# Fronts beside four plain MLP groups, then eight groups with both MLP layers as Strassen's seven products: one change to a lightning-attention and Fourier-mix kernel

## The chip, the cores and the metric

The kernel runs on one core of a Trainium2 chip. The metric is the device time of one execution in microseconds (us), lower is better. Three runs before the change took 942.44, 943.5 and 944.67 us; the median is 943.5 us.

## The reference, cut to what matters

B is 4 sequences of S = 768 rows, H = 8 heads of D = 64, so that the bridge gives x of 4 x 768 x 512. All is float32.

```
# attention, in blocks of 64 rows, a state per head carried along
intra = (q_b k_b^T * Dmask) v_b ;  inter = (q_b * lam^(i+1)) state
state = lam^64 * state + (k_b * rev_pow)^T v_b
x     = heads side by side                      # 4 x 768 x 512
# Fourier mix and MLP
u  = x + real(fft2(x))                          # over the 768 rows and 512 columns
un = (u - mean(u)) / sqrt(var(u) + 1e-6)
out = u + max(un @ w1, 0) @ w2                  # w1: 512 x 2048, w2: 2048 x 512
```

## The kernel before, in words

**Fronts.** For each sequence b a front makes the input of the MLP. `attn_chunk` works on 128 rows at a time (NC = 6 chunks): three loads, transposes of k and q (L259, L264), scores (L277), the state (L292 to L297), the output (L305, L309) and its transposes (L316). PSUM tiles of the fronts come from the pool `pa` with 5 buffers. `fft_ln` then writes and gathers mirrored rows through DRAM (`mirror_a`, `mirror_b`, L364 to L372), folds them on VectorE (`fold_a`, `fold_b`, L352 to L403), does the transform over rows (L427) and over columns (`width`, L440 to L445), adds it to x (L490, L491) and, for each of the three groups of a sequence, normalizes (`norm`: L457 to L469), transposes (L473) and copies the result to `ut` (L474). `ut` has 2 buffers, the row tiles `x` have 10. A group g is the pair of 128-row tiles (g, 3 + g); the groups come in the order 1, 2, 0.

**MLP.** `mlp(b)` goes over the three groups of a sequence. Layer 1 (L513): 16 chunks of 128 hidden units, each the sum of 4 products of 128x128 weights with 128x256 of `ut`; ReLU alternates between ScalarE (L521) and VectorE (L519) and fills the tiles `hr`. Layer 2 (L527): for both row tiles 16 products of a 128x128 of `hr` with 128x512 of w2. Two additions (L533, L534) make `y`, which is stored plainly or, for the upper row tile, scattered (L538). PSUM of the MLP comes from the pool `pm` with 3 buffers. Every matmul of the program stands as two instructions in the trace, since it is float32.

**Order.** Front and MLP are generators that yield a guessed cost after each step. `weave(lead, other, ratio)` writes the program: after each step of `lead` it takes steps of `other` until their cost is `ratio` times that of the lead. The Tile framework then plans the order on each engine ahead of time: among the instructions whose inputs and buffers its own model has ready, it takes the one that was written first, and each engine runs its queue in that order. Front 0 is woven with the conversion of the weights, its transform with front 1, the rest of front 1 with the MLP of sequence 0 (ratio 1.5). Fronts 2 and 3 are each woven with the MLP of the sequence ahead (`0.9 * t_mlp / t_front`, about 2.0); the MLP of sequence 3 stands alone.

Of the kernel before, what the change touches and what calls it, by code (L numbers as in the profile page):

```python
# [75 lines left out]
def kernel(  # L76
# [25 lines left out]
    G = 2  # L102
    NG = NC // G
    TT = [(t, HC + t) for t in range(HC)]
# [5 lines left out]
    ld = ctx.enter_context(tc.tile_pool(name="ld", bufs=2))  # L110
    at = ctx.enter_context(tc.tile_pool(name="at", bufs=1))
    xp = ctx.enter_context(tc.tile_pool(name="xp", bufs=2 * NC - 2))
    xn = ctx.enter_context(tc.tile_pool(name="xn", bufs=HC))
    fp = ctx.enter_context(tc.tile_pool(name="fp", bufs=1))
    np_ = ctx.enter_context(tc.tile_pool(name="np", bufs=2))
    ep = ctx.enter_context(tc.tile_pool(name="ep", bufs=2))
    hp_ = ctx.enter_context(tc.tile_pool(name="hp", bufs=FO // 4 + 1))
    dram = ctx.enter_context(tc.tile_pool(name="dram", bufs=1, space=bass.MemoryType.DRAM))
    PS = bass.MemoryType.PSUM
    pa = ctx.enter_context(tc.tile_pool(name="pa", bufs=5, space=PS))  # L120
    pm = ctx.enter_context(tc.tile_pool(name="pm", bufs=3, space=PS))
# [21 lines left out]
    n, b2 = 1, 0  # L143
    while n < C:
# [3 lines left out]
        n, b2 = 2 * n, b2 + 1  # L148
# [21 lines left out]
    for g in range(0, H, 4):  # L170
        ps = psum_m([C, 4, C])
# [12 lines left out]

    cs = const.tile([128, 2, 2, 2, NK], F32, name="cs")
    dt = const.tile([128, 5, QM + 1], F32, name="dt")
    ix = const.tile([128, 2 + HC * (B + 1)], U32, name="ix")

    def row_of(j, n=128):
        return bass.IndirectOffsetOnAxis(ap=ix[0:n, j:j + 1], axis=0)  # L190

    w1 = const.tile([128, KO, DFF], F32, name="w1")
    w2 = const.tile([128, FO, DM], F32, name="w2")

    w1v = moe_w_ch1.rearrange("(c p) f -> p c f", p=128)
    w2v = moe_w_ch2.rearrange("(c p) m -> p c m", p=128)
# [42 lines left out]
    xs, xn_, xd = {}, {}, {}  # L239
# [95 lines left out]

    uts = {}
# [75 lines left out]
    def fft_ln(b):  # L414
# [7 lines left out]
        for i in range(5):  # L422
            ps = psum_a([128, 2, NK])
            m = 128 if i < 4 else 1
            for n in range(2):
                for a, rows in enumerate(BLK):
                    mm = nc.tensor.matmul(ps[0:m, n, :], lhsT=piece(a, i, n), rhs=cs[0:rows, a, i in (2, 3), n, :],  # L427
                                          start=(a == 0), stop=(a == 1))
# [24 lines left out]
        def norm(g):  # L453
            mv = new(np_, [128, G, 2], "mv")
            for i in range(G):
                stt = new(np_, [128, 6], "stt")
                nc.vector.bn_stats(stt, xs[b, TT[g][i]])  # L457
                nc.vector.bn_aggr(mv[:, i, :], stt)
            ve = new(np_, [128, G], "ve")
            rs = new(np_, [128, G], "rs")  # L460
            nc.gpsimd.tensor_scalar(ve, mv[:, :, 1], EPS, None, op0=ALU.add)
            nc.gpsimd.tensor_tensor(rs, ve, mhalf, op=ALU.pow)
            yield 1.0
            ut = uts[b, g] = new(np_, [128, KO, G * 128], "ut")
            for i in range(G):
                un = new(np_, [128, DM], "un", bufs=1)
                u = xs[b, TT[g][i]]
                for o, x in ((un[:, 0:HM], u[:, 0:HM]), (un[:, HM:DM], u[:, DM - 1:HM - 1:-1])):
                    nc.vector.tensor_scalar(o, x, mv[:, i, 0:1], rs[:, i:i + 1],  # L469
                                            op0=ALU.subtract, op1=ALU.mult)  # L470
                pt = psum_a([128, KO, 128])
                for c in range(KO):
                    nc.tensor.transpose(pt[:, c, :], un[:, 128 * c:128 * c + 128], ident)  # L473
                nc.scalar.copy(ut[:, :, 128 * i:128 * i + 128], pt)  # L474
                yield 0.7

        for t in (1, 2, 0):
            ps = psum_a([128, DM])
# [3 lines left out]
            B = bs[t % 2]  # L482
# [6 lines left out]
            u, v_ = xs[b, t], xs[b, HC + t]  # L489
# [3 lines left out]
            if t == 0:  # L493
                ps = psum_a([128, DM])
# [8 lines left out]
            yield from norm(t)  # L503


    def mlp(b):
        for g in (1, 2, 0):
            ut = uts.pop((b, g))
            hr = []
            for fc in range(FO):  # L510
                ps = psum_m([128, G * 128])
                for c in range(KO):
                    nc.tensor.matmul(ps, lhsT=w1[:, c, 128 * fc:128 * fc + 128], rhs=ut[:, c, :],  # L513
                                     start=(c == 0), stop=(c == KO - 1))
                if fc % 4 == 0:
                    hr.append(new(hp_, [128, 4, G * 128], "hr"))
                t = hr[-1][:, fc % 4, :]
                if fc % 2:
                    nc.vector.tensor_scalar(t, ps, 0.0, None, op0=ALU.max)  # L519
                else:  # L520
                    nc.scalar.activation(t, ps, AF.Relu)  # L521
                yield 1.7
            for i in range(G):
                T = TT[g][i]
                ps = psum_m([128, DM])
                for fc in range(FO):
                    nc.tensor.matmul(ps, lhsT=hr[fc // 4][:, fc % 4, 128 * i:128 * i + 128], rhs=w2[:, fc, :],  # L527
                                     start=(fc == 0), stop=(fc == FO - 1))
                    if fc % 4 == 3 and fc < FO - 1:
                        yield 3.4  # L530
                u = xs.pop((b, T))
                y = new(np_, [128, DM], "y", bufs=1)
                nc.vector.tensor_tensor(y[:, 0:HM], ps[:, 0:HM], u[:, 0:HM], op=ALU.add)  # L533
                nc.vector.tensor_tensor(y[:, HM:DM], ps[:, HM:DM], u[:, DM - 1:HM - 1:-1], op=ALU.add)  # L534
                if T < HC:
                    nc.sync.dma_start(out[b, 128 * T:128 * T + 128, :], y)
                else:
                    nc.gpsimd.indirect_dma_start(out=out.rearrange("b s d -> (b s) d"),  # L538
                                                 out_offset=row_of(2 + HC * (b + 1) + T - HC),
                                                 in_=y[:, :], in_offset=None)  # L540
                yield 3.4
# [24 lines left out]
    def run(gen):  # L566
        return sum(gen)

    def part(gen, n):
        for d in gen:  # L570
            yield d
            n -= d
            if n <= 0:
                return

    NW = KO * DFF // WP
    w = weights()
    t_mlp = NG * (FO * 1.7 + G * 4 * 3.4)
    t_chunk = 7.3
    t_att, t_front = NC * t_chunk, NC * t_chunk + 10.0 + 7.0 + 5.7 + 3 * 2.4  # L580
    run(weave(attn(0), part(w, 0.5 * NW), 0.5 * NW / t_att))
# [9 lines left out]
    for b in range(B):  # L591
        back = mlp(b)
        if b == 0:

            run(weave(part(fr, 2 * t_chunk), weave(part(back, FO * 1.7 - 1.0), w, 0.9), 1.5))
            run(w)
# [34 lines left out]
```

## Time and profile before

| what | value |
|---|---|
| median of 3 runs | 943.5 us |
| the profiled execution, its own time | 942.13 us |
| its span, first to last instruction | 940.4 us |
| granted TensorE clock, mean of the span | 0.983 |
| matmul busy (PE) | 868.4 us |
| VectorE, ScalarE, GpSimd busy | 314.9, 184.7, 95.7 us |
| layer 1 matmuls (L513), layer 2 matmuls (L527) busy | 350.3, 336.8 us |
| DMA moved | 55.59 MB |

A group line of the page reads: line, engine, operation, output tile <- input tiles, shapes, count | busy time and mean of one | idle time of the engine ahead of them and what ended most of it. In a timeline a row is start, duration, engine, line, operation, count of merged instructions, and in brackets the idle time ahead of it with what ended it. The duration of merged matmuls reaches to the modelled end of the last, which overlaps the next row; distances between starts are used for rates. In the chain of waits a row is start, length, engine and line.

### The profile page before, as it was taken

The page shows a single profiled execution, that of the slowest core. Times are in us where ns is not written, and L with a number is a line of the kernel's source. Part 1 is how long each engine was busy: PE and PEld are TensorE (multiplying, and loading weights), DVE is VectorE, ACT ScalarE, POOL GpSimd, SP SyncE. Part 2 cuts the span into 40 slices and gives each one's busy share as a digit, 9 for nine tenths or more (in the row PEclk, how much of TensorE's full clock was granted, in tenths as well). Part 3 has the DMA queues.
Part 4 walks back from the last instruction along what each step waited for, and adds up shares of the span by engine and source line. Part 5 has one row for each costly group of instructions (what it writes and reads, how often), then busy time and mean ns, then how long its engine had stood idle before and what let it go on. Part 6 is the DMA issues. An engine that isn't in the chain of part 4 may idle for free.

```text
span 940.4 us, 10700 instructions
## 1 busy us (share of the span) xinstructions
PE 868.4 (92%) x4404; PEld 597.6 (64%) x4404; DVE 314.9 (33%) x694; ACT 184.7 (20%) x403; POOL 95.7 (10%) x108
## 2 busy tenths in 40 slices
PE   4766687699999999999999999999999999999997
PEld 2655576547747668668668558658668658485763
DVE  4779879843601011112243412111242401010100
ACT  3665346701100002112012001112002001000000
POOL 2225412000100001011100001010200000000000
PEclk9998889899999999999999999999999999999999
DMA  9798417500000011222200011221200000000000
GB/s 223 213 240 252 134 46 219 157 22 23 1 12 12 1 45 37 55 79 73 79 23 0 1 45 34 57 65 38 62 23 1 1 23 0 12 12 11 12 0 23
DMA packets 89272, 55.59 MB, mean 59 GB/s; under 512 B 76768, under 2 KB 78312, under 8 KB 89224
## 3 DMA queue, kind: packets, MB, share of 16 engines
q1 hardware_dynamic: 83264, 40.73, 16.5%
q0 software_dynamic: 2496, 7.87, 2.5%
q10 hardware_dynamic: 3464, 6.30, 1.8%
q8 instruction: 35, 0.57, 0.3%
q14 instruction: 13, 0.11, 0.0%
HBM read 42.29 MB, written 12.60 MB: 58 GB/s over the span
## 4 chain that ended last, share of the span: by engine, by line
PE 76%; DVE 10%; issue 4%; DMA 4%; ACT 2%; POOL 1%; POOLq 0%; SPq 0%; DVEq 0%; ACTq 0%
PE pm L527 32%; PE pm L513 29%; PE pa L427 3%; DMA raw<-in_moe_w_ch_dram 3%; PE pa L309 2%; PE pa L277 2%; PE pa L473 1%; PE pa L305 1%; PE pa L316 1%; DVE pw L222 1%; DVE stt L457 1%; DMA r<-xa,ix 1%; PE pa L292 1%; PE pa L264 1%; PE pa L259 1%
## 5 line engine op out<-in xcount | busy, mean ns | idle before, releaser
L513 PE MATMUL pm<-ut,w 128*128 128x256 f32 x1536 | 350.3, 383 | 9.8 <-ACT hr L521 8.0
L527 PE MATMUL pm<-w,hr 128*128 128x512 f32 x768 | 336.8, 594 | 0.0
L513 PEld LDWEIGHTS pm<-ut,w 128*128 128x128 f32 x1536 | 287.5, 191 | 54.9 <-ACT hr L521 8.7
L527 PEld LDWEIGHTS pm<-w,hr 128*128 128x128 f32 x768 | 143.7, 190 | 168.3 <-issue 167.4
L519 DVE TENSOR_SCALAR hr<-pm 128x256 f32<-128x256 f32 x96 | 40.7, 423 | 234.6 <-PE pm L513 234.3
L521 ACT ACTIVATE hr<-pm 128x256 f32<-128x256 f32 x96 | 36.7, 384 | 385.6 <-PE pm L513 354.1
L533 DVE TENSOR_TENSOR y<-pm,x 128x256 f32<-128x256 f32 x24 | 10.2, 425 | 234.9 <-PE pm L527 234.9
L538 POOL DMA_INDIRECT out_dram<-y,ix x12 | 12.1, 1009 | 344.0 <-DVE y L534 343.7
L255 POOL TENSOR_TENSOR kd<-k,decay 128x512 f32<-128x512 f32 x20 | 25.8, 1290 | 190.6 <-issue 110.7
L309 PE MATMUL pa<-sc,v 128*64 128x128 f32 x384 | 31.6, 292 | 10.5 <-DVE sc L281 10.5
L281 DVE TENSOR_TENSOR sc<-pa,decay 128x512 f32<-128x512 f32 x48 | 31.3, 685 | 24.8 <-PE pa L277 21.3
L277 PE MATMUL pa<-qT,kT 64*128 64x128 f32 x384 | 30.2, 298 | 8.9 <-ACT qT L266 8.9
L277 PEld LDWEIGHTS pa<-qT,kT 64*128 64x128 f32 x384 | 25.2, 199 | 18.1 <-ACT qT L266 11.9
L309 PEld LDWEIGHTS pa<-sc,v 128*64 128x64 f32 x384 | 23.5, 144 | 17.5 <-DVE sc L281 13.6
L269 DVE TENSOR_TENSOR qs<-pa,qpow 128x512 f32<-128x512 f32 x20 | 13.8, 691 | 48.4 <-ACT qT L266 48.4
L312 ACT COPY oT<-pa 128x512 f32<-128x512 f32 x24 | 14.1, 585 | 78.9 <-PE pa L309 78.9
L473 PE MATMUL pa<-ident,un 128*128 128x128 f32 x96 | 16.6, 294 | 13.6 <-DVE un L469 13.6
L261 ACT COPY kT<-pa 128x512 f32<-128x512 f32 x24 | 14.1, 588 | 72.5 <-PE pa L259 72.1
L220 ACT ACTIVATE pw<-pw,cvt 128x512 uint16<-128x512 uint16 x32 | 22.8, 719 | 17.1 <-DVE pw L219 17.1
L305 PE MATMUL pa<-qs,st 64*64 64x128 f32 x320 | 22.7, 283 | 3.2 <-DVE qs L269 3.1
L473 PEld LDWEIGHTS pa<-ident,un 128*128 128x128 f32 x96 | 11.3, 146 | 22.0 <-issue 12.4
L296 POOL TENSOR_TENSOR st<-st,qpow 128x256 f32<-128x256 f32 x16 | 22.5, 1406 | 19.0 <-DVE st L297 10.2
(94 smaller groups left out, 641.5 us busy)
## 6 DMA issues: line engine op xcount, KB each, us to landing
raw<-in_moe_w_ch_dram SPq DMA_DIRECT2D x32, 512.0 KB, 4.8
k<-in_k_dram SPq DMA_DIRECT2D x24, 256.0 KB, 3.4
q<-in_q_dram SPq DMA_DIRECT2D x24, 256.0 KB, 3.8
v<-in_v_dram SPq DMA_DIRECT2D x24, 256.0 KB, 3.1
out_dram<-y SPq DMA_DIRECT2D x12, 256.0 KB, 2.0
xa<-x ACTq DMA_DIRECT2D x8, 256.0 KB, 3.0
xa<-xn ACTq DMA_DIRECT2D x8, 256.0 KB, 4.4
xb<-xn ACTq DMA_DIRECT2D x8, 256.0 KB, 6.1
```

What stands on the lines that cost most here:

```text
L220: nc.scalar.activation(pw, pw, AF.Relu, bias=cvt[:, 0:1], scale=-1.0)
L255: nc.gpsimd.tensor_tensor(kd, kt, kpow, op=ALU.mult)
L277: mm(pss[hi][:, hp, :], lhsT=kT[HD[hi], hp, :], rhs=qT[HD[hi], hp, :], start=True, stop=True)
L281: nc.vector.tensor_tensor(t, pss[hi], decay[:, hi::2, :], op=ALU.mult)
L305: mm(po[HD[hi], hp, :], lhsT=s_old[HD[hi], hp, :], rhs=qs[HD[hi], hp, :], start=(hp == 0), stop=False, skip_group_check=True)
L309: mm(po[HD[hi], hp, :], lhsT=vt[:, 2 * hp + hi, :], rhs=sc[hi][:, hp, :], start=(c == 0 and hp == 0), stop=(hp == HP - 1), skip_group_chec ...
L427: mm = nc.tensor.matmul(ps[0:m, n, :], lhsT=piece(a, i, n), rhs=cs[0:rows, a, i in (2, 3), n, :], start=(a == 0), stop=(a == 1))
L473: nc.tensor.transpose(pt[:, c, :], un[:, 128 * c:128 * c + 128], ident)
L513: nc.tensor.matmul(ps, lhsT=w1[:, c, 128 * fc:128 * fc + 128], rhs=ut[:, c, :], start=(c == 0), stop=(c == KO - 1))
L519: nc.vector.tensor_scalar(t, ps, 0.0, None, op0=ALU.max)
L521: nc.scalar.activation(t, ps, AF.Relu)
L527: nc.tensor.matmul(ps, lhsT=hr[fc // 4][:, fc % 4, 128 * i:128 * i + 128], rhs=w2[:, fc, :], start=(fc == 0), stop=(fc == FO - 1))
```

## The change

The MLP runs in two ways. The first four groups in order, `PLAIN` = (0,1), (0,2), (0,0), (1,1), go as before, one generator per group. All that is left of fronts 1, 2 and 3 is chained and woven beside them. For the other eight groups, `LATE`, the front stores `ut` and the two row tiles to DRAM. When the fronts end, their pools are closed, and sums of weights and the loads of the stored tiles take their memory, each new tile waiting for the old tiles under it (`reuse_waits="tile"`).

The late groups go in four pairs. Both layers of a pair are Strassen's scheme in Winograd's form: seven products of half-size blocks for eight. In layer 1 the blocks are halves of the 512 inputs and of the 2048 hidden units, and the two groups; in layer 2 halves of the hidden units and of the 512 outputs, and the two groups. Sums of weight blocks are made once (`combine_weights`: eight of them, each in two VectorE additions of 1024 columns; two overwrite parts of w1 and w2 and so follow the plain groups), sums of input blocks once per pair, sums of hidden blocks in `finish`. The running sums of Winograd's form are kept in PSUM: a product is added to bank X behind a copy of what X held. All 8 banks serve the late part.

```diff
-    const = ctx.enter_context(tc.tile_pool(name="const", bufs=1))
...
+    const = front_pool("const", 1)
...
+    xp = plain_pool("xp", 2 * NC - 2)
+    up = plain_pool("up", 2)
+    hp_ = plain_pool("hp", FO // 4 + 1)
...
-            ut = uts[b, g] = new(np_, [128, KO, G * 128], "ut")
+            ut = new(up, [128, KO, G * 128], "ut")
...
+            if (b, g) in PLAIN:
+                uts[b, g] = ut
+                return
+            utd[b, g] = dram.tile([128, KO, G * 128], F32, name=f"utd{b}{g}")
+            nc.sync.dma_start(utd[b, g], ut)
+            for T in TT[g]:
+                ud[b, T] = dram.tile([128, DM], F32, name=f"ud{b}{T}")
+                nc.sync.dma_start(ud[b, T], xs.pop((b, T)))
...
+    ORDER = [(b, g) for b in range(B) for g in (1, 2, 0)]
+    PLAIN, LATE = ORDER[:4], ORDER[4:]
...
+    def combine_weights(part):
...
+            todo = [(ws[:, 0], a21, a22, ADD), (ws[:, 1], ws[:, 0], a11, SUB), (ws[:, 2], a12, ws[:, 1], SUB),
+                    (wz[:, 0], b12, b11, SUB), (wz[:, 1], b22, wz[:, 0], SUB), (wz[:, 2], b21, wz[:, 1], SUB)]
+        else:
...
+            todo = [(a21, a11, a21, SUB), (b12, b22, b12, SUB)]
...
+        for o, x, y, op in todo:
+            n = o.shape[1]
+            for i in range(0, n, n // 2):
+                V.tensor_tensor(o[:, i:i + n // 2], x[:, i:i + n // 2], y[:, i:i + n // 2], op=op)
+                yield 1.3
+    def load_u(j):
+        r = s2.u[j] = new(s2.up, [128, 2, KO, G * 128], "ur", bufs=2)
+        for h, (b, g) in enumerate(LATE[2 * j:2 * j + 2]):
+            nc.sync.dma_start(r[:, h], utd[b, g])
+    def late(j):
...
+        V.tensor_tensor(t[:, 0], b12, b11, op=SUB)
+        V.tensor_tensor(t[:, 1], b22, t[:, 0], op=SUB)
+        V.tensor_tensor(t[:, 2], b21, t[:, 1], op=SUB)
+        V.tensor_tensor(b12, b22, b12, op=SUB)
...
+        def prod(ps, a, b, i, first):
+            for kt in range(2):
+                nc.tensor.matmul(ps, lhsT=s2.A[a][:, kt, 128 * i:128 * i + 128], rhs=U[b][:, kt, :],
+                                 start=(first and kt == 0), stop=(kt == 1), skip_group_check=True)
...
+        def finish(i, X, Z):
...
+            prod(X, "s4", "b22", i, False)
+            a21 = new(s2.hp, [128, G, 128], "a21", bufs=2)
+            nc.scalar.activation(a21, two(X), AF.Relu)
+            prod(Z, "a22", "t4", i, False)
+            V.tensor_tensor(a12, two(Z), a12, op=ADD)
+            V.tensor_scalar(a12, a12, 0.0, None, op0=ALU.max)
+            V.tensor_tensor(s1, a21, a22, op=ADD)
+            V.tensor_tensor(s2_, s1, a11, op=SUB)
+            V.tensor_tensor(s3, a11, a21, op=SUB)
+            V.tensor_tensor(s4, a12, s2_, op=SUB)
+        last = None
+        for i in range(HF):
...
+            prod(X, "a11", "b11", i, True)
+            nc.scalar.copy(a11, two(X))
+            prod(Y, "a12", "b21", i, True)
+            V.tensor_tensor(a11, two(Y), a11, op=ADD)
+            V.tensor_scalar(a11, a11, 0.0, None, op0=ALU.max)
+            if last:
+                finish(*last)
+            prod(X, "s2", "t2", i, False)
+            nc.scalar.copy(a12, two(X))
+            prod(Z, "s3", "t3", i, True)
+            prod(X, "s1", "t1", i, False)
+            nc.scalar.copy(a22, two(X))
+            V.tensor_tensor(a22, two(Z), a22, op=ADD)
+            V.tensor_scalar(a22, a22, 0.0, None, op0=ALU.max)
+            last = (i, X, Z)
+        finish(*last)
+        if 2 * j + 2 < len(LATE):
+            load_u(j + 1)
+        def prod2(ps, a, b, s, first):
+            for i in range(HF):
+                nc.tensor.matmul(ps, lhsT=h[a][:, s, i, :], rhs=s2.B[b][:, i, :],
+                                 start=(first and i == 0), stop=(i == HF - 1), skip_group_check=True)
...
+            prod2(X, "s1", "t1", s, False)
+            V.tensor_tensor(y[1][:, hi], X, us[1][:, rev], op=ADD)
+            V.tensor_tensor(y[1][:, hi], Z, y[1][:, hi], op=ADD)
+            prod2(X, "s4", "b22", s, False)
+            V.tensor_tensor(y[0][:, hi], X, us[0][:, rev], op=ADD)
+            store(*who[0], y[0])
+            prod2(Z, "a22", "t4", s, False)
...
-    fr, mix = front(1), fft_ln(0)
+    fr, mix = chain(front(b) for b in range(1, B)), fft_ln(0)
...
-            run(weave(fr, back, 1.5))
-        elif b + 1 < B:
-            run(weave(front(b + 1), back, 0.9 * t_mlp / t_front))
-        run(back)
+    back = chain(mlp(b, g) for b, g in PLAIN)
+    run(weave(part(fr, 2 * t_chunk), weave(part(back, FO * 1.7 - 1.0), w, 0.9), 1.5))
+    run(w)
+    t_rest = 3 * t_front - 6 * t_chunk
+    run(weave(fr, back, (len(PLAIN) * t_mlp - FO * 1.7 - 25.0) / t_rest))
+    front_end.close()
...
+    load_u(0)
+    run(weave(combine_weights(0), back, 1.5))
+    run(back)
+    plain_end.close()
+    psums.close()
...
+    run(combine_weights(1))
+    for j in range(len(LATE) // 2):
+        late(j)
```

More of the change, by code (lines that the diff above doesn't have):

```diff
@@ L332, in attn_chunk @@
         yield 1.7
-    uts = {}
+    uts, utd, ud = {}, {}, {}
     ys = [const.tile([128, 2 * NK], F32, name=f"ys{i}") for i in range(5)]
@@ L503, in fft_ln @@
             yield from norm(t)
[L506 to L509, printed above, removed]
-            for fc in range(FO):
[L511 to L541, printed above, removed]
@@ new lines, with store, mlp @@
+    ORDER = [(b, g) for b in range(B) for g in (1, 2, 0)]
+    PLAIN, LATE = ORDER[:4], ORDER[4:]
+    def store(b, T, y):
+        if T < HC:
+            nc.sync.dma_start(out[b, 128 * T:128 * T + 128, :], y)
+        else:
+            nc.gpsimd.indirect_dma_start(out=out.rearrange("b s d -> (b s) d"),
+                                         out_offset=row_of(2 + HC * (b + 1) + T - HC),
+                                         in_=y[:, :], in_offset=None)
+    def mlp(b, g):
+        ut = uts.pop((b, g))
+        hr = []
+        for fc in range(FO):
+            ps = psum_m([128, G * 128])
+            for c in range(KO):
+                nc.tensor.matmul(ps, lhsT=w1[:, c, 128 * fc:128 * fc + 128], rhs=ut[:, c, :],
+                                 start=(c == 0), stop=(c == KO - 1))
+            if fc % 4 == 0:
+                hr.append(new(hp_, [128, 4, G * 128], "hr"))
+            t = hr[-1][:, fc % 4, :]
+            if fc % 2:
+                nc.vector.tensor_scalar(t, ps, 0.0, None, op0=ALU.max)
+            else:
+                nc.scalar.activation(t, ps, AF.Relu)
+            yield 1.7
+        for i in range(G):
+            T = TT[g][i]
+            ps = psum_m([128, DM])
+            for fc in range(FO):
+                nc.tensor.matmul(ps, lhsT=hr[fc // 4][:, fc % 4, 128 * i:128 * i + 128], rhs=w2[:, fc, :],
+                                 start=(fc == 0), stop=(fc == FO - 1))
+                if fc % 4 == 3 and fc < FO - 1:
+                    yield 3.4
+            u = xs.pop((b, T))
+            y = new(up, [128, DM], "y", bufs=1)
+            nc.vector.tensor_tensor(y[:, 0:HM], ps[:, 0:HM], u[:, 0:HM], op=ALU.add)
+            nc.vector.tensor_tensor(y[:, HM:DM], ps[:, HM:DM], u[:, DM - 1:HM - 1:-1], op=ALU.add)
+            store(b, T, y)
+            yield 3.4
@@ L590 @@
     run(weave(mix, weave(part(fr, 1.5 * t_chunk), part(w, 0.3 * NW), 0.3 * NW / 11.0), 0.5))
[L591 to L596, printed above, removed]
-            run(weave(fr, back, 1.5))
-        elif b + 1 < B:
-            run(weave(front(b + 1), back, 0.9 * t_mlp / t_front))
-        run(back)
+    back = chain(mlp(b, g) for b, g in PLAIN)
[4 more added lines that the diff above has]
+    front_end.close()
+    s2.wp = ctx.enter_context(tc.tile_pool(name="ws", bufs=1, side="left", reuse_waits="tile"))
+    s2.up = ctx.enter_context(tc.tile_pool(name="us", bufs=1, side="left", reuse_waits="tile"))
+    s2.u = {}
+    load_u(0)
[3 more added lines that the diff above has]
+    psums.close()
+    s2.hp = ctx.enter_context(tc.tile_pool(name="h2", bufs=1, side="right", reuse_waits="tile"))
+    s2.yp = ctx.enter_context(tc.tile_pool(name="y2", bufs=1, side="right", reuse_waits="tile"))
+    s2.ps = ctx.enter_context(tc.tile_pool(name="p2", bufs=8, space=PS, reuse_waits="tile"))
+    run(combine_weights(1))
+    for j in range(len(LATE) // 2):
+        late(j)
 _INS = ['q', 'k', 'v', 'lam', 'moe_w_ch1', 'moe_w_ch2']
```

84 lines of the change are left out of this document (70 added, 14 removed).

## The prediction, made before the changed kernel was run

> **What bounds the kernel now.** I read the page's busy times and slices first.
>
> ```profile
> span 940.4 us, 10700 instructions
> ...
> PE 868.4 (92%) x4404; PEld 597.6 (64%) x4404; DVE 314.9 (33%) x694; ACT 184.7 (20%) x403; POOL 95.7 (10%) x108
> ...
> PE   4766687699999999999999999999999999999997
> PEld 2655576547747668668668558658668658485763
> DVE  4779879843601011112243412111242401010100
> ```
>
> TensorE is the bound from the ninth slice on (about 210 us): its row is all nines, and VectorE stands at 0 to 4. Ahead of that VectorE (7 to 9) and the weights' conversion set the pace; the change leaves that part as it is. So time is won only by fewer matmuls, and lost only where TensorE comes to wait. Next I took the rate of the matmuls from the chain of waits, where the MLP stands without a front:
>
> ```profile
> 287.46 27.63 PE pm L513 x128
> 315.09 27.47 PE pm L527 x64
> ...
> 906.76 13.75 PE pm L527 x32
> 920.51 0.02 issue
> 920.54 0.42 DVE y L533
> ```
>
> Layer 1 of a group is 128 instructions in 27.63 us, 0.216 us each at 256 columns; layer 2 is 64 in 27.47, 0.429 each at 512 columns, 0.215 per 256. A group is 55.10 us. Last, what a front adds: front 2 begins, and front 3 begins, with these transposes.
>
> ```profile
> 342.39 0.60 PE L259 MATMUL pa<-ident,k 128*128 128x128 f32 x4
> ...
> 460.27 24.20 PE L527 MATMUL pm<-w,hr 128*128 128x512 f32 x56
> ...
> 555.59 0.60 PE L259 MATMUL pa<-ident,k 128*128 128x128 f32 x4
> ```
>
> Between them lie 213.2 us and exactly the three groups of sequence 1, 165.3 us. A front costs TensorE 47.9 us. Its six attention chunks end at 460.27, when a group, a layer 1 and 8 of 64 instructions of a layer 2 have run (55.1 + 27.6 + 3.4 = 86.1): 117.9 - 86.1 = 31.8 us for the chunks, 16.1 for the transform and norm.
>
> **Part two, the seven products.** A plain pair of groups is 110.2 us. A late pair has in layer 1 8 rows of hidden blocks x 7 products x 2 matmuls x 2 instructions = 224, in layer 2 2 x 7 x 8 x 2 = 224, all at 256 columns: 448 x 0.216 = 96.7 us. Four pairs save 4 x 13.5 = 53.9 us. This takes the layer 1 rate for layer 2 as well; the row that bears on it:
>
> ```profile
> L513 PEld LDWEIGHTS pm<-ut,w 128*128 128x128 f32 x1536 | 287.5, 191 | 54.9 <-ACT hr L521 8.7 <-issue 6.5 <-DVE hr L519 2.1
> L519 DVE TENSOR_SCALAR hr<-pm 128x256 f32<-128x256 f32 x96 | 40.7, 423 | 234.6 <-PE pm L513 234.3
> L521 ACT ACTIVATE hr<-pm 128x256 f32<-128x256 f32 x96 | 36.7, 384 | 385.6 <-PE pm L513 354.1
> ```
>
> A weight load takes 0.191 us and hides beside a matmul of 0.216, as it does in layer 1 now.
>
> The Trainium skill (TensorE: Matmul & The Clock Gate, section Back-to-back issue gap) speaks against this half of the change: it gives sustained spacings of about 81 ns at 128 columns and 131 ns at 512, so that halving the columns should cost far more than nothing per column. Estimated from that page, 256 columns would lie near 98 ns, and layer 2 would take 1.5 times as long per column as now. The trace disagrees: 0.216 against 0.429 us, a ratio of 0.503.
>
> What replaces the matmuls is small instructions on VectorE and ScalarE. Their price comes from SBUF additions of the fold and of the transforms' end:
>
> ```profile
> 471.45 0.68 DVE L352 TENSOR_TENSOR fe<-x,x 128x512 f32<-128x512 f32 x1
> 472.05 0.68 DVE L353 TENSOR_TENSOR fo<-x,x 128x512 f32<-128x512 f32 x1
> ...
> 474.34 0.42 DVE L396 TENSOR_TENSOR fe<-fe 128x256 f32<-128x256 f32 x1
> 474.67 0.42 DVE L397 TENSOR_TENSOR fe<-fe 128x256 f32<-128x256 f32 x1
> ```
>
> Start to start that is 0.60 us at 512 columns and 0.33 at 256, so I estimate 1.13 at 1024. Per hidden block in layer 1 VectorE does 10 operations of 256 columns, 3.4 us, and ScalarE 4 of 0.38; TensorE needs 28 x 0.216 = 6.05 us. VectorE is busy 56% and not the bound. The waits are bound by position: bank X is copied out and at once used again. The tightest place in layer 1 is the copy of `a12`, covered by one other product, 4 x 0.216 = 0.86 us. The round trip is 0.03 us from the last matmul to the eviction (920.51 to 920.54), 0.38 for the copy, and about 0.15 back (the first half of `un` at 510.09 + 0.42 lets TensorE start at 510.65, rows below): 0.56 us, covered by 0.3 us to spare. In layer 2 `s4` follows `s1` in X with nothing written between: 0.03 + 0.42 + 0.15 = 0.6 us, 8 times, 4.8 us, unless the planner puts the next tile's first product there, which it can for all but the last. No row shows such re-use of a bank, so the late part costs between 0 and 15 us (all 8 places and 0.3 us at each of 32 blocks); I take 3, nearest to the covered round trip.
>
> **Part one, the fronts beside four groups.** Fronts 2 and 3 had about 2.0 us of MLP written behind each us of front; now all fronts have (4 x 54.4 - 27.2 - 25)/177.3 = 0.93. What cover do they need? The norm step first, on TensorE and on VectorE:
>
> ```profile
> 504.37 5.35 PE L513 MATMUL pm<-ut,w 128*128 128x256 f32 x24
> 510.65 0.67 PE L473 MATMUL pa<-ident,un 128*128 128x128 f32 x4 [0.94 <-DVE un L469]
> ```
> ```profile
> 510.09 0.73 DVE L469 TENSOR_SCALAR un<-x,mv,rs 128x256 f32<-128x256 f32 x2 [1.16 <-POOL rs L462]
> ```
>
> From the last matmul of `width` (the 24 of the MLP follow it) to the transposes the chain takes 6.3 us, of which 5.35 were covered and 0.94 waited. By the weave alone the cover of the 1.6 + 1.0 units written there falls from 5.2 to 2.4 us (a unit is about 1 us: a group counts 54.4 and takes 55.1), a wait of 3.9. Then the fold, from the last chunk's transposes (460.3):
>
> ```profile
> 465.20 0.95 POOL L372 DMA_INDIRECT x<-xb,ix  x1 [0.30 <-issue]
> ```
> ```profile
> x<-xb,ix POOLq DMA_INDIRECT x8, 3.4
> ```
> ```profile
> 480.49 0.41 DVE L403 TENSOR_TENSOR fo<-fo 65x256 f32<-65x256 f32 x1
> ```
>
> The gather lands at 468.6; the fold took 471.45 to 480.9, 9.5 us, behind an eviction; alone it would end at 478.1, 17.8 us behind the transposes, against 24 us of cover before and 11.7 x 0.93 = 10.9 written now: a wait of 6.9. If TensorE ran in written order, fronts 2 and 3 would lose 6 x 3.9 + 2 x 6.9 = 37 us; front 1, woven at 1.5 before, about 3 x 1.5 + 4 = 8; and twelve chunks, each with 6.8 us of matmuls among five evictions, perhaps 1 us each: 57 us in all. But the planner doesn't keep to the written order:
>
> ```profile
> POOL x L372 <- DVE y L534: 53.6, 2, 37.7
> ```
> ```profile
> 211.98 6.28 PE L527 MATMUL pm<-w,hr 128*128 128x512 f32 x14
> 218.09 6.64 PE L513 MATMUL pm<-ut,w 128*128 128x256 f32 x30
> 224.95 3.31 PE L427 MATMUL pa<-cs,fe 65*1 65x193 f32 x18 [0.22 <-DVE fe L392]
> ```
>
> Front 1's second gather had to wait for a row tile that the first group's `y` freed, and 44 later MLP instructions were put into the gap; the transform came 0.22 us late. So a front that is held up costs TensorE nothing while plain matmuls are left, and front 1's new ratio changes nothing. What stays is what the planner misjudges, like the 0.94 at each norm. Between 0 (the cover found) and 57 I take 8, nearest to these rows: some 4 more for each of fronts 2 and 3.
>
> Enough cover is left if the fronts' shortest chain ends ahead of TensorE's sum. When layer 2 of group (0,2) ends (287.46, where the next layer 1 begins), 110.2 us of plain matmuls and two fronts, 95.8, remain: TensorE gets through at 493. The fronts are held up by `ut`, still two buffers:
>
> ```profile
> 259.56 1.07 ACT L474 COPY ut<-pa 128x512 f32<-128x512 f32 x2 [1.34 <-PE pm L513]
> ```
>
> The transposed tiles of (1,1) waited in PSUM until layer 1 of (0,2) had ended. After the change (1,1) keeps one buffer until the last plain group, so (1,2) and (1,0) hold four of the five `pa` buffers until layer 1 of (0,0) ends, 27.6 us on, at 315. Suppose front 2 stood still until then: its chunks at TensorE's own 31.8, its transform and norm uncovered some 50 (17.8, then 7 of transform matmuls, three steps of 7.4, the rest in PSUM waits), front 3's chunks mostly in those gaps (15 left over), its transform 50: 315 + 147 = 462, 31 us ahead of 493. The program leaves 25.
>
> The stored tiles add 8 x 2 MB (512 + 2 x 256 KB, out and in) to 55.59 MB. SyncE's queue holds the next chunk's loads behind a store that waits for `ut`; a chunk of lead (`ld` has two buffers) hides that, and the engines are a third busy in the busiest part:
>
> ```profile
> 400.00:450.00 50.00, 50.00 (x317) 36.68 (x316) 9.86 (x20) 8.74 (x21) 6.66 (x7) 1.00 0.32 87
> ```
>
> **The hand-over.** The weight sums lie over the fronts' buffers and can't begin before front 3's last transposes: 12 x 1.13 = 13.6 us of VectorE, then 4 x 0.60 = 2.4 for the sums of the first pair. Its input's load is a 512 KB transfer like these:
>
> ```profile
> raw<-in_moe_w_ch_dram SPq DMA_DIRECT2D x32, 512.0 KB, 4.8
> ```
>
> Uncovered that is 13.6 + 2.4 + 4.8 = 21 us; with the plain matmuls that should be left, nothing, except that `b12` and the evictions queue on VectorE behind the last plain additions while TensorE has the first two products of two or three blocks (some 5 us) to run. Between 0 and 21 I take 5.
>
> **The sum.** The span is 940.4 us, this run's time 942.1, the median 1.4 more: 943.5 - 53.9 = 889.6, + 8 + 5 + 3 = 905.6. I say 905 us. A measurement of this kernel can tell about 0.2% (2 us) from no change.
>
> **The rivals.** *Fronts run out of cover* (still faster). If front 3's chain ends after the plain matmuls, half of the 57 and 15 to 21 of the hand-over come due: 889.6 + 28 + 15 to 21 = 933 to 939. For it: 0.93 is less than half of the cover before. Against: 31 us of slack. *TensorE keeps to the written order* (slower). The place is every norm and fold of the fronts, the price 57, and with the matmuls used up the hand-over's 21: 889.6 + 57 + 21 + 3 = 971. It decides when over 30 us of the 57 come due beside the 21 and the 3. Such gaps also cost clock:
>
> ```profile
> 75.00:100.00 25.00, 14.82 (x143) 12.02 (x143) 23.95 (x48) 9.40 (x19) 14.25 (x7) 0.77 0.63 179
> ```
>
> With TensorE 59% busy the granted clock fell to 0.77. The Trainium skill (TensorE: Matmul & The Clock Gate, section HAM oscillation — how this bites in real kernels) puts it as half clock after idle gaps beyond about 3.4 us; this row agrees in direction. Against this rival stand the rows at 211.98. *Products wait for evictions* (slower). If the three re-uses of X in a block each expose 0.6 us, that is 32 x 3 x 0.6 = 58: 889.6 + 8 + 5 + 58 + 5 = 966; it decides from a round trip of some 1.4 us where I count 0.56. *Weight loads no longer hide* (slower). At 0.191 for each of the 96 added loads of a pair's layer 2, 73 us: 979; against it stands layer 1. The spacing rule of the Trainium skill would lead here, too. *Nothing is saved*: waits of 54 us by chance, or products that take longer for changing banks each four instructions: 943.
>
> **How the numbers follow.** Forecast, 888 to 925: 0.68. Out of cover: 0.17. Written order 0.06, evictions 0.05, weight loads 0.02, nothing saved 0.02. Faster is 0.85, same 0.02, slower 0.13. The range goes from 887 (the sum without added waits, less the 2 us that the two late fronts' norms wait now) to 935, into the second case, and leaves the slower ones out.
>
> **What would show it.** L513 down to a third with 0.216 us each, and the late products at 0.216 in both layers; TensorE nines through the fronts, granted clock 1.00; waits at L473 of about 1 us; front 3's last transposes 15 us or more ahead of the last plain layer 2; a gap at the hand-over of at most some 5 us; a late pair from start to start in 97 to 98. I would be wrong if slices of the fronts' stage fell below 9, if the late products showed idle time behind ScalarE or VectorE in each block, or if a product took over 0.22.

## The result, and the profile after

The changed kernel takes 909.3 us, the median of four runs from 908.4 to 911.4, against 943.4 beside it: a ratio of 0.964, interval 0.962 to 0.966. That is 34 us saved, where 905 us was forecast. The profiled execution took 908.43 us with a span of 906.4. These are its page's busy times, slices and one group of the late products:

```profile
span 906.4 us, 11761 instructions
...
PE 826.5 (91%) x4660; PEld 652.9 (72%) x4660; DVE 437.0 (48%) x1006; ACT 209.0 (23%) x467; POOL 90.7 (10%) x108
...
PE   4775678699999999999999899999999999999997
...
DVE  4779869854532135443567756115531454135410
...
L627 PE MATMUL p<-ur,w 128*128 128x256 f32 x384 | 95.1, 382 | 3.3 <-DVE ur L620 1.9
```

TensorE still bounds the kernel: nines with one 8, in the slice where the plain groups hand over to the late ones (507.69 us). VectorE has gone from 33% to 48% and is nowhere near full behind the fronts. TensorE has more instructions than before and 42 us less busy time. The busy column of a group counts overlapping matmuls twice; rates come from starts, here from the chain of waits in the late part:

```profile
610.80 45.76 PE p L627 x212
...
707.49 45.76 PE p L627 x212
...
804.19 45.76 PE p L627 x212
```

A late pair is 96.69 us from start to start (804.19 - 707.49 = 96.70, 707.49 - 610.80 = 96.69), where two plain groups take 110.2. Nothing in the chain but matmuls stands between two pairs. TensorE's timeline shows where the rest went; front 2's chunks, the start of front 3, the hand-over and the end:

```profile
261.01 0.65 PE L272 MATMUL pa<-ident,k 128*128 128x128 f32 x4
...
286.99 0.66 PE L272 MATMUL pa<-ident,k 128*128 128x128 f32 x4
...
290.63 1.16 PE L290 MATMUL pa<-qT,kT 64*128 64x128 f32 x8
291.71 1.13 PE L559 MATMUL pm<-w,hr 128*128 128x512 f32 x2
292.77 1.16 PE L290 MATMUL pa<-qT,kT 64*128 64x128 f32 x8
...
300.93 0.65 PE L272 MATMUL pa<-ident,k 128*128 128x128 f32 x4
...
337.65 1.16 PE L290 MATMUL pa<-qT,kT 64*128 64x128 f32 x8 [1.70 <-DVE sc L294]
...
396.08 0.60 PE L272 MATMUL pa<-ident,k 128*128 128x128 f32 x4
...
403.09 0.60 PE L272 MATMUL pa<-ident,k 128*128 128x128 f32 x4
...
405.78 1.16 PE L290 MATMUL pa<-qT,kT 64*128 64x128 f32 x16
...
410.93 0.60 PE L272 MATMUL pa<-ident,k 128*128 128x128 f32 x4
...
491.38 16.47 PE L559 MATMUL pm<-w,hr 128*128 128x512 f32 x38
507.69 1.03 PE L627 MATMUL p<-ur,w 128*128 128x256 f32 x4
510.16 1.10 PE L627 MATMUL p<-ur,w 128*128 128x256 f32 x4 [1.45 <-DVE y L566]
513.14 1.22 PE L627 MATMUL p<-ur,w 128*128 128x256 f32 x2 [1.87 <-DVE ur L620]
...
893.63 3.72 PE L674 MATMUL p<-w,hs 128*128 128x256 f32 x16 [0.52 <-DVE y L695]
897.19 3.62 PE L674 MATMUL p<-w2s,ha 128*128 128x256 f32 x16
```

Read in three stretches:

- The last plain product ends at 507.69. The prediction's sum without waits was 287.46 + 110.2 + 95.8 = 493.5, so the fronts cost 14.2 us. Its estimate was 8.
- From there four pairs alone would take 4 x 96.7 = 386.8 us, to 894.5. The last matmul ends at 897.19 + 3.45 = 900.6 (16 x 0.216). So 6.1 us are lost, nearly all in the first pair behind 507.69; the estimate was 5 + 3.
- 5.8 us follow behind the last matmul, against 6.2 before (the last layer 2 there ends at 934.2 by TensorE's timeline, the span at 940.4).

In spans: 940.4 - 53.9 = 886.5; 886.5 + 14.2 + 6.1 - 0.4 = 906.4.

Which front was it? Front 2's transposes begin at 261.01 and front 3's at 396.08: 135.07 us, with 128 layer 1 instructions (27.6) and 108 of layer 2 (46.4) in it. That leaves 61.1 us for a front which cost 47.9 before. Front 3, up to 491.38, leaves 48.8. So front 2 carries 13.2 of the 14.2 us. One of its chunks goes from 286.99 to 300.93: 13.94 us with 16 layer 2 instructions (6.86 us) in it, 7.08 us of TensorE for a chunk. A chunk of front 3, 403.09 to 410.93, shows 7.84 with six such instructions (2.58): 5.26 us, as before the change (31.8 / 6 = 5.3). In front 2 the 16 score products (L290) stand in two eights with MLP products between; in front 3 they stand in one row of 16. Six chunks at 1.8 us more make 10.8 of the 13.2 us; waits such as 1.70 us for the scores of the last chunk make part of the rest.

Why front 2 runs in pieces stands in ScalarE's timeline, in the copies out of the `pa` buffers into `ut`:

```profile
360.98 1.07 ACT L487 COPY ut<-pa 128x512 f32<-128x512 f32 x2 [1.34 <-PE pm L545]
364.98 1.07 ACT L487 COPY ut<-pa 128x512 f32<-128x512 f32 x2
```

The transposes of (1,2) and (1,0) had run by 261.01. Their copies, two PSUM tiles each, come at 360.98, when layer 1 of (0,0) has ended, and at 364.98. So four of the five buffers were held through all six chunks (261.01 to 345.31), and 46 us past the 315 that the prediction counted on. No load held these chunks back behind a store that waits for `ut`: SyncE issued loads of k, q and v all that time (261.74 to 344.01) and the first such store only at 362.07.

### The profile page after: what moved, and what is told of

It is laid out like the page before. It is cut to its first block, busy times and chain, and to the rows that moved or that the text cites. A ratio compares the mean times of both kernels' runs of the same rounds, so it can differ in the third digit from the quotient of the medians.

```text
span 906.4 us, 11761 instructions
## 1 busy us (share of the span) xinstructions
PE 826.5 (91%) x4660; PEld 652.9 (72%) x4660; DVE 437.0 (48%) x1006; ACT 209.0 (23%) x467; POOL 90.7 (10%) x108
## 4 chain that ended last, share of the span: by engine, by line
PE 51%; DVE 5%; issue 1%; DMA 1%; POOL 1%; ACT 0%; POOLq 0%; DVEq 0%; ACTq 0%
PE p L627 21%; PE p L674 21%; PE pm L545 1%; PE pm L559 1%; PE pa L440 1%; PE pa L486 1%; PE pa L290 1%; PE pa L322 1%; DVE stt L470 1%; DVE w1s L604 1%; DVE w2s L604 1%; PE pa L318 1%; POOL rs L475 0%; DVE x L512 0%; DVE x L513 0%
## 5 line engine op out<-in xcount | busy, mean ns | idle before, releaser
L545 PE MATMUL pm<-ut,w 128*128 128x256 f32 x512 | 124.2, 392 | 10.0 <-ACT hr L553 8.2
L559 PE MATMUL pm<-w,hr 128*128 128x512 f32 x256 | 120.6, 602 | 0.0
L545 PEld LDWEIGHTS pm<-ut,w 128*128 128x128 f32 x512 | 95.9, 194 | 26.3 <-ACT hr L553 8.9
L627 PE MATMUL p<-ur,w 128*128 128x256 f32 x384 | 95.1, 382 | 3.3 <-DVE ur L620 1.9
L627 PEld LDWEIGHTS p<-ur,w 128*128 128x128 f32 x384 | 73.3, 191 | 14.5 <-issue 2.3
L559 PEld LDWEIGHTS pm<-w,hr 128*128 128x128 f32 x256 | 44.8, 190 | 40.3 <-issue 38.8
L627 PE MATMUL p<-us,w1s 128*128 128x256 f32 x256 | 66.6, 383 | 0.0
L674 PE MATMUL p<-w,hs 128*128 128x256 f32 x256 | 58.0, 379 | 0.5 <-DVE y L695 0.5
L674 PE MATMUL p<-w2s,hs 128*128 128x256 f32 x256 | 57.9, 379 | 0.0
L674 PE MATMUL p<-w,ha 128*128 128x256 f32 x256 | 57.9, 379 | 0.0
L290 PEld LDWEIGHTS pa<-qT,kT 64*128 64x128 f32 x384 | 30.1, 193 | 25.9 <-ACT qT L279 14.4
L290 PE MATMUL pa<-qT,kT 64*128 64x128 f32 x384 | 36.2, 291 | 11.7 <-ACT qT L279 10.0
L294 DVE TENSOR_TENSOR sc<-pa,decay 128x512 f32<-128x512 f32 x48 | 31.8, 684 | 29.1 <-PE pa L290 26.3
```

Source lines behind the costliest of these rows:

```text
L290: mm(pss[hi][:, hp, :], lhsT=kT[HD[hi], hp, :], rhs=qT[HD[hi], hp, :], start=True, stop=True)
L294: nc.vector.tensor_tensor(t, pss[hi], decay[:, hi::2, :], op=ALU.mult)
L627: nc.tensor.matmul(ps, lhsT=s2.A[a][:, kt, 128 * i:128 * i + 128], rhs=U[b][:, kt, :], start=(first and kt == 0), stop=(kt == 1), skip_gro ...
L674: nc.tensor.matmul(ps, lhsT=h[a][:, s, i, :], rhs=s2.B[b][:, i, :], start=(first and i == 0), stop=(i == HF - 1), skip_group_check=True)
```

## The experiments

The theory after the first trace: the seven products bring the whole 53.9 us; front 2 runs slow because the transposed tiles of (1,2) and (1,0) hold four of the five `pa` buffers until `ut` comes free, so its steps queue for one buffer, come in small pieces, and cost TensorE time; VectorE's queue opens the gap of the hand-over. Ratios are to the kernel before, run beside these versions: 944.15 us for the first four, 943.53 for the last three.

### Part one alone

The late groups are loaded back and run by the plain MLP; none of the seven products is made.

```diff
-        ut = uts.pop((b, g))
+        if (b, g) in PLAIN:
+            ut = uts.pop((b, g))
+        else:
+            ut = new(up, [128, KO, G * 128], "ut")
+            nc.sync.dma_start(ut, utd[b, g])
+            for T in TT[g]:
+                xs[b, T] = new(xp, [128, DM], "x")
+                nc.sync.dma_start(xs[b, T], ud[b, T])
...
-    for j in range(len(LATE) // 2):
-        late(j)
+    run(chain(mlp(b, g) for b, g in LATE))
```

> Part one alone: all fronts beside four plain groups, the other eight groups stored, loaded back and computed by the plain MLP, no Strassen products. Theory (the seven products save exactly 53.9 us of matmuls, all else of the change costs about 20): after's 909.3 + 53.9, less the 5 to 6 us that the sums of weights cost at the hand-over and 0.5 of waits in the late part: 956 to 959 us, so slower than before by 13 to 15, nearly all of it in front 2. Rival (the fronts are covered as well as before, and the seven products fall short of 53.9 by their own waits): 943 to 948.

It took 956.9 us, ratio 1.014 (1.010 to 1.018), as the theory said: part one alone makes the kernel 1.4% slower. Its chain of waits, where the plain groups end:

```profile
494.91 13.30 PE pm L566 x31
508.21 27.63 PE pm L552 x128
```

The fourth group ends at 508.2, as in the changed kernel, and layer 1 of the fifth follows with no gap. The span is 14.5 us above the one before: what part one costs is the fronts' 14 us, and the loads back cost nothing. The step to the changed kernel, 956.9 - 909.3 = 47.6, is part two: 53.9 less the 6 of the hand-over.

### The late `ut` tiles in the fold's buffers

```diff
-            ut = new(up, [128, KO, G * 128], "ut")
+            ut = new(*((up, [128, KO, G * 128], "ut") if (b, g) in PLAIN else
+                       (fp, [128, KO, G * 128], ("fe0", "fo0", "fe1")[g])))
```

> After, but the transposed tile of a late group goes into a buffer of the fold that is idle by then, so it doesn't wait for a plain group's layer 1 and frees its PSUM buffers at once. Theory (front 2 costs TensorE 13 us more than in before because its chunks run on one PSUM buffer): front 2 from 61 to 48 to 50 us, the time 897 to 900. Rival (the front stage loses its 14 us because less matmul work stands between the fronts' steps, whatever the buffers): 907 to 910.

It took 890.5 us, ratio 0.944 (0.941 to 0.947), 7 us under what the theory said. TensorE's timeline: first a row of front 1 in the changed kernel, then in this version the same row, front 2, and the end of the plain groups:

```profile
209.53 0.90 PE L440 MATMUL pa<-cs,fe 128*128 128x193 f32 x4 [1.38 <-DVE fe L409]
```
```profile
206.99 0.90 PE L440 MATMUL pa<-cs,fe 128*128 128x193 f32 x4 [1.52 <-DVE fe L409]
...
272.07 0.60 PE L272 MATMUL pa<-ident,k 128*128 128x128 f32 x4
...
274.75 1.16 PE L290 MATMUL pa<-qT,kT 64*128 64x128 f32 x16
...
279.90 0.60 PE L272 MATMUL pa<-ident,k 128*128 128x128 f32 x4
...
317.44 1.63 PE L440 MATMUL pa<-cs,fe 128*128 128x193 f32 x4 [2.77 <-DVE fe L409]
...
467.74 27.63 PE L560 MATMUL pm<-w,hr 128*128 128x512 f32 x64
495.20 3.19 PE L628 MATMUL p<-ur,w 128*128 128x256 f32 x14
```

A chunk of front 2 now takes 7.83 us with six layer 2 instructions in it, 5.25 of its own: front 3's price. Front 2 as a whole costs 51.9 us instead of 61.1, where 48 to 50 were expected; 2.77 of it is a wait at its fold. The plain groups end at 495.20, 12.5 us sooner. Not all of that is the edit's: 9.2 us are front 2's and 0.9 front 3's, but 2.5 stand there already at the transform of front 1 (206.99 against 209.53), which the edit does not touch, and are scatter between two executions. The other part I had missed: the fronts end some 32 us ahead of the plain groups instead of 16, VectorE has the weight sums done in time, and the first pair starts at 495.20 without a gap. 12.5 and the first pair's 5.5 make 18.0; the spans differ by 906.4 - 888.5 = 17.9. So the held `pa` buffers are shown as the cause of most of the fronts' loss, 10 of 14 us, and, through the shorter lead, of the hand-over's.

### The scores in order of the array's halves

The 16 score products of a chunk have 64 rows each and alternate between the two row halves of the array. Here they come by half; everything else is as in the changed kernel.

```diff
-        for hp in range(HP):
-            for hi in range(2):
+        for hi in range(2):
+            for hp in range(HP):
```

> After, with the score products written one half of the heads after the other in every chunk, as the single PSUM buffer forced it in front 2 only. Theory (products on the two 64-row halves of the array run side by side when they alternate, 16 instructions in 1.09 us, and one after the other when they don't, 2.17): front 3 grows by 6 x 1.08 = 6.5 us; fronts 0 and 1, where TensorE isn't the bound all the time, by 0 to 8 in all: 916 to 923. Rival (the 2.17 us in front 2 were a wait for the buffer, not the order): 908 to 911.

It took 912.4 us, 3.1 more than the changed kernel, between both expectations, so that neither holds in full. TensorE's timeline, a chunk of front 3:

```profile
404.01 0.60 PE L272 MATMUL pa<-ident,k 128*128 128x128 f32 x4
...
406.69 1.71 PE L290 MATMUL pa<-qT,kT 64*128 64x128 f32 x16
...
412.39 0.60 PE L272 MATMUL pa<-ident,k 128*128 128x128 f32 x4
```

By half, 16 score instructions take 1.64 us; alternating they took 1.09 (405.78 to 406.87 in the changed kernel). The chunk grows from 7.84 to 8.38, and six chunks of front 3 give 3.3 us: the whole difference. The theory had taken front 2's two times 1.08 us for the price of one half after the other; in a run that price is 1.64. Front 2 loses nothing more (from start to start it is even 1.7 us shorter, after a start 1.8 us later), because its two eights already are one per half: 1.08 us each (290.63 to 291.71), 2.16 against 1.09. Of that 1.07 us, 0.55 is the halves no longer working side by side. The other half is the break itself: eight of one half take 0.82 in a run (1.64 / 2) and 1.08 between MLP products. So the scores explain 1.07 of the 1.8 us per chunk; the other 0.7 lies at the breaks between the other steps, which I did not take apart.

### The sums of w2 later

`wz` and the overwritten `b12` are first needed in layer 2 of the first pair. Here they are made behind its layer 1.

```diff
-                    (wz[:, 0], b12, b11, SUB), (wz[:, 1], b22, wz[:, 0], SUB), (wz[:, 2], b21, wz[:, 1], SUB)]
...
-            todo = [(a21, a11, a21, SUB), (b12, b22, b12, SUB)]
+            todo = [(a21, a11, a21, SUB)] if part == 1 else [
+                (wz[:, 0], b12, b11, SUB), (wz[:, 1], b22, wz[:, 0], SUB), (wz[:, 2], b21, wz[:, 1], SUB),
+                (b12, b22, b12, SUB)]
...
+        if j == 0:
+            run(combine_weights(2))
```

> After, with the four sums of blocks of w2 (8 additions of 1.13 us) written behind layer 1 of the first late pair instead of ahead of it. Theory (the 5 to 6 us lost at the hand-over are the input sums queued on VectorE behind 16 weight additions): the gap goes to at most 1 us, 903 to 905. Rival (TensorE waits there for the last plain groups' additions and the new PSUM buffers anyway): 907 to 909.

It took 903.3 us, ratio 0.956 (0.953 to 0.959), as the theory said. First VectorE's timeline of the changed kernel at the hand-over, then TensorE's of this one:

```profile
505.87 3.48 DVE L604 TENSOR_TENSOR w<-w 128x1024 f32<-128x1024 f32 x3
...
509.94 1.21 DVE L604 TENSOR_TENSOR w<-w 128x1024 f32<-128x1024 f32 x1
511.07 0.68 DVE L617 TENSOR_TENSOR us<-ur 128x512 f32<-128x512 f32 x1
...
512.39 0.69 DVE L620 TENSOR_TENSOR ur<-ur 128x512 f32<-128x512 f32 x1
```
```profile
510.40 1.03 PE L628 MATMUL p<-ur,w 128*128 128x256 f32 x4
511.89 1.32 PE L628 MATMUL p<-ur,w 128*128 128x256 f32 x5 [0.46 <-DVE y L566]
```

In the changed kernel VectorE makes four weight sums (1.14 us each from start to start; the prediction's estimate was 1.13) in the last 5 us ahead of the sums of the pair's input, and TensorE's longest wait there, 1.87 us, is for the input sum at L620. With the sums of w2 moved, about 0.6 us remain of 5.5. The hand-over is VectorE's queue and not the loads; the memory given over can account for no more than those 0.6. The edit moves the sums of `wz` and `b12` together, so it does not tell their shares apart. The profiled execution of this version (span 904.4) was the slowest of five and 2.4 us late already at the transform of front 1, so the gap is read from the rows and not from the spans.

### Two plain groups, five late pairs

Added to the version with `ut` in the fold's buffers: a fifth pair saves another 13.5 us, if the fronts find cover beside two plain groups.

```diff
-    PLAIN, LATE = ORDER[:4], ORDER[4:]
+    PLAIN, LATE = ORDER[:2], ORDER[2:]
```

> The kernel of e2 (late transposes in the fold's buffers) with two plain groups instead of four and ten late ones. Theory (the fronts cost TensorE nothing beyond their own matmuls only while plain matmuls last; without them their chain shows): the plain matmuls end 110 us earlier, the fronts' chain of two folds, six norm steps and the chunks doesn't; fronts end at 400 to 415 us of the span, the sums of weights and the first loads come uncovered behind them, five late pairs of 96.7 follow: 905 to 915 us. Rival (cover isn't what matters, TensorE's sum is): 890.5 less one pair's 13.5: 876 to 879.

It took 940.4 us, ratio 0.998 (0.996 to 1.001): 50 us more than with four plain groups, so the rival is out, and some 25 above the theory. Rows of TensorE's timeline, then of its windows (span of the stretch; busy of PE, its loads, VectorE, ScalarE, GpSimd; granted clock; DMA share; GB/s):

```profile
386.88 1.62 PE L440 MATMUL pa<-cs,fe 128*128 128x193 f32 x4 [10.49 <-DVE fe L409]
...
402.67 1.08 PE L487 MATMUL pa<-ident,un 128*128 128x128 f32 x4 [5.79 <-DVE un L483]
...
447.34 2.04 PE L628 MATMUL p<-us,w1s 128*128 128x256 f32 x4 [10.20 <-DVE us L619]
```
```profile
376.00:400.00 24.00, 10.36 (x54) 8.22 (x52) 15.77 (x37) 4.08 (x12) 2.24 (x3) 0.79 0.16 50
400.00:430.00 30.00, 11.32 (x50) 9.05 (x50) 15.69 (x38) 4.51 (x12) 2.81 (x6) 0.62 0.26 101
430.00:450.00 20.00, 6.41 (x14) 4.70 (x15) 18.60 (x20) 0.74 (x2) 0.00 (x0) 0.50 0.41 149
```

This is what lack of cover looks like: 10.5 us at the fold, 5.8 at a norm (the prediction had 6.3 for that chain uncovered), then some 20 us from 427 to 447 for the hand-over (predicted uncovered: 21). The prices of the norm and the hand-over held. The fold's did not: the prediction had 17.8 us from the last transposes to the end of the whole fold, but the transform here starts 11.1 us behind them (375.74 to 386.88), at the first folded part. What the expectation had too low was the end of the fronts, 427 us where it had 400 to 415, and I had also summed its own parts 5 to 10 us too low. A price it left out is the clock: with TensorE busy 32 to 43% of the stretch the granted clock fell to 0.50 to 0.79, and four transposes take 1.08 us instead of 0.60. The Trainium skill (TensorE: Matmul & The Clock Gate, section HAM oscillation — how this bites in real kernels) gives half clock after idle gaps beyond about 3.4 us; the 0.50 in the stretch with gaps of 6.0 and 10.2 us agrees.

### One copy made three times

Also on the version with `ut` in the fold's buffers. It measures how much room the tightest re-use of bank X has.

```diff
-            nc.scalar.copy(a12, two(X))
+            for _ in range(3):
+                nc.scalar.copy(a12, two(X))
```

> The kernel of e2 with the tightest copy of the late part (bank X to a12, with one product between it and the next use of X) made three times, two of them for nothing. Theory (the round trip of 0.03 + 0.38 + 0.15 = 0.56 us lies under the 0.86 us of the product between): with about 0.6 us more it sticks out by 0.3 at each of 32 blocks where the planner finds no other product to put there: 890 to 900. Rival 1 (the evictions bind already, some waits are hidden in the 96.7 us of a pair): 32 x 0.6 = 19 us more, 909 or over. Rival 2 (evictions are far from binding, ScalarE has room for both): 889 to 892; then this place has over 0.6 us to spare, and my count of it is too tight.

It took 901.7 us, ratio 0.954 (0.951 to 0.958), 1.7 us above the theory's range and clear of both rivals. The chain of waits, then ScalarE's and TensorE's timelines at one such place:

```profile
601.28 46.60 PE p L628 x208
...
699.92 46.60 PE p L628 x208
```
```profile
516.98 1.18 ACT L663 COPY ha<-p 128x256 f32<-128x256 f32 x3 [1.34 <-PE p L628]
```
```profile
516.78 1.46 PE L628 MATMUL p<-ur,w 128*128 128x256 f32 x6
```

A pair grew from 96.69 to 98.64 us: 1.95 in 8 hidden blocks, 0.24 us per block (1.95 / 8). Three copies take 1.18 us (0.40 more for each added one). That makes the round trip 0.56 + 0.80 = 1.36 us. The cover grew as well: behind the product that is copied, six instructions (1.30 us) now come ahead of the next use of X, where the version without the edit has four (0.86); the planner had put half of another product there. By this count 0.06 us should show and 0.24 does, so a single copy is hidden, but with some 0.1 us to spare rather than the 0.3 of the prediction; this is an estimate. If the evictions bound already, a block would show all that is added beyond the added cover, 0.80 - 0.44 = 0.36 us, and a pair 2.9; it grew by 1.95, so rival 1 is out.

The four pairs account for 7.8 of the 11 us between the two medians. The two profiled executions lie 14.2 us apart, and the other 6 stand ahead of 150 us, where both kernels have the same order of instructions. In the three stretches of 25 us from 75 to 150 the granted clock was 0.57, 0.70 and 0.91 here, against 0.70, 0.82 and 1.00 without the edit; that the lower clock is the cause is not shown. So I rest on the length of the pair alone.

### The last store plain

Also on the version with `ut` in the fold's buffers: the upper row tile, whose store is scattered, is finished ahead of the lower one in layer 2 of a pair.

```diff
-        for s in range(G):
+        for s in reversed(range(G)):
```

> The kernel of e2 with the upper row tile of every late pair first, so that the last stores of the kernel are plain ones and not scattered. Theory (the end of the span is the last scatter's issue and landing, 5.6 us behind the last matmul): a plain store of 256 KB lands in about 2 us from its issue, against 2.8 and about 1 us of GpSimd's work: 888 to 889.5. Rival (the end is the program's own, whatever the last store): 890 to 891.

It took 888.9 us, ratio 0.942 (0.939 to 0.946), the best version here. The ends, without the edit and with it:

```profile
882.96 0.42 DVE L702 TENSOR_TENSOR y<-p,y 128x256 f32<-128x256 f32 x1 [3.03 <-PE p L675]
883.69 0.96 POOL L536 DMA_INDIRECT out_dram<-y,ix  x1 [2.52 <-DVE y L702]
```
```profile
880.44 3.79 SPq L534 DMA_DIRECT2D out_dram<-y  x2
...
883.44 0.42 DVE L702 TENSOR_TENSOR y<-p,y 128x256 f32<-128x256 f32 x1 [3.03 <-PE p L675]
```

Behind the start of the last addition the end came after 3.4 us (886.8 - 883.44) instead of 5.5 (888.5 - 882.96). One to 2.5 us were expected and 1.7 lie between the medians, which is near the scatter of the runs; the rows show it better than the times. Against the changed kernel this version is 20 us faster, nearly all by the edit of one buffer.

## Why the prediction was right or wrong

**Part two was right to a tenth.** "Four pairs save 4 x 13.5 = 53.9 us": 96.69 us per pair against 96.7. The term rested on one choice, the layer 1 rate for products that now have 256 columns instead of 512. The late products run at 0.216 us in both layers, and the weight loads stay hidden. So the spacing rule that the prediction weighed there did not hold for this kernel, and the rival "weight loads no longer hide" (979) is out.

**The rivals.** *Products wait for evictions* is out: no pair shows such waits, and the copy made three times shows the round trip fits, with less to spare than was counted. *TensorE keeps to the written order* is out by the nines through the fronts. *Fronts run out of cover* did not happen with four plain groups: front 3's last transposes lie 16.3 us ahead of 507.69, where 15 or more were forecast. With two groups it did happen, and the prices of single steps (5.8 for 6.3, 20 for 21) show that the mechanism was real, though the fold's price, 17.8, was some 7 us too high. Four groups are enough, two are not. *Nothing is saved* is out.

**The term that was mis-sized is the fronts': 8 us forecast, 14.2 measured.** The step is "Suppose front 2 stood still until then". I had seen that (1,2) and (1,0) would hold four of the five `pa` buffers, counted the delay, found it inside the lead, and so priced it at nothing. But front 2 did not stand still, and the buffers came free at 361 to 365 and not at 315. It ran on the one buffer left, each chunk in many small pieces between MLP products, and that costs time on TensorE, which no lead covers: 1.8 us per chunk, some 11 us in all. "A front that is held up costs TensorE nothing while plain matmuls are left" is the sentence that fell. With the buffers freed front 2 costs 4.0 us more than the 47.9 instead of 13.2, and front 3 nothing.

**The hand-over was right in size.** 5 forecast, 5.5 lost, and the cause named there, VectorE's queue, is the one that moving the sums confirmed; besides `b12` and the evictions, the sums that overwrite part of w1 stood in it. What I did not see is that it hangs on the same buffers: with 32 us of lead it is gone. **The late waits** were taken at 3 and cost 0.5: the planner put the next tile's first product into the re-use of X everywhere but at the last tile, the row at 893.63.

So the sum missed by 4 us, 6 too little for the fronts and 2.5 too much for the late waits; that the two errors partly cancel is luck. Left open: what exactly a break costs in front 2's chunks outside the scores (0.7 us each), and why the same row of front 1's transform comes anywhere from 207 to 214 us in executions that have the same order of instructions up to it.

## What to carry to other kernels

A held buffer is not only a delay. When an engine that is the bound fills the delay with pieces of other work, ask what each piece costs more than in a run, and look who keeps the buffers: here the place of one tile was worth 19 us, beside 48 for eight rewritten groups. Cover is a stock that several users draw on: the 16 us of lead that the freed buffers gave also hid the hand-over, and taking two plain groups away cost 50 us, nearly the 53 that the change had won with the buffers freed.

## What the runs showed of the hardware that was not expected

Products of 64 rows that alternate between the two row halves of the array run partly side by side: 16 instructions in 1.09 us, against 1.64 by half, a factor of 1.5. One such instruction over all 128 rows, a transpose, takes 0.11 (four from 403.09 to 403.53), so that 16 one after another would take 1.7, and only the alternating ones are clearly faster. The Trainium skill (TensorE: Matmul & The Clock Gate, section Part 3: Packing small matmuls — row/col tiling) says that products in different row groups run at the same time; the runs agree, but short of a factor of 2, and only where the two halves stand next to each other in the queue. Eight of one half between full-size products took 1.08 us, as long as all 16 in a run.
